# RetNet attention and a multiplicative FFN on one core: attention of the later batches in chunks of 64 positions on array quarters, placed inside the items

## The chip, the core and the metric

The kernel runs on one core of a Trainium2 chip. The metric is the device time of one execution in microseconds. In the text TensorE is PE (PEld: its weight loads), VectorE is DVE, ScalarE is ACT, GpSimd is POOL, and SyncE is SP; PSUM is the accumulator memory, in banks of 2 KB a partition.

## The reference

Everything is float32. Attention has 8 batches, 8 heads, 576 positions and 64 channels a head; the rows of its result go through an FFN with products.

```
scores = q @ k.T / sqrt(64)                     # per batch and head
Dmat   = where(i >= j, gamma[h] ** (i - j), 0)  # decay, gamma[h] = 1 - 2**(-5-h)
x      = ((scores * Dmat) @ v) -> (4608, 512)   # rows: batch, position; columns: head, channel
out    = ((x @ w1) * (x @ w2)) @ w3 @ w_out     # w1, w2: 512x1024; w3: 1024x1024; w_out: 1024x512
```

## The kernel before

**Attention.** Two batches (a pair) go together, and the 576 positions are cut into five chunks: one of 64 and four of 128. A chunk of a pair is a *unit*; there are 20, unit 0 to 4 for the first pair, 5 to 9, 10 to 14 and 15 to 19 for the others. The decay is taken apart: q is multiplied by a power of gamma, v by its inverse (`scale_blocks`, `scale`), so that only a triangular 0/1 mask is left within a chunk, and what earlier chunks give is a running sum over k times v, the *state*. Per unit TensorE has four steps of 16 matmuls each (two batches, eight heads):

- `score` (L233): k times q of the chunk, two heads at once on two halves of the array's rows, into PSUM tiles `sc`; VectorE multiplies them by the mask into `pm` (L236).
- `state` (L255): k times v is added to the PSUM tile `st`, on two halves of the columns; ScalarE copies `st` to SBUF as `sb` (L259), for the next unit. The last chunk of a pair has none.
- `pv_state` (L274): `sb` times q into the PSUM tiles `xps`, on four quarters of the array, 64 by 64 each. The first chunk of a pair has none.
- `pv` (L299): v times `pm` is added to `xps`, on two halves of the columns; ScalarE copies `xps` to the token tile `xT` (L306).

**FFN.** Its products are made by Strassen's scheme. Three kinds of *items* stand in a list `todo`, and `work(n)` issues the next n: `up` (L524, seven products of 8 records of 192 columns; x times w1 and w2 for the first two pairs' tokens), `up2` (L1028, seven of 4 records; two levels of the scheme, for the later pairs, with weight forms that are kept in HBM as `kept` and come back through a ring `ra`), and `down` (L637, seven products of 8 records of 256 columns; the result times w3 times w_out, which was multiplied once before). A matmul in float32 is two records in the trace. GpSimd makes the token forms that `up2` needs (`token_forms`, L948) and some sums (L1033); VectorE adds products up (L1040), multiplies a with b (L1003), and transposes blocks of q and k (L190). `up2` leaves one product outstanding, which `finish` issues inside the next item. An item takes lists of small work with it: `aside` (transposes), `beside` (scaling v on ScalarE), `loads`.

**Order.** The order on every engine is the order of the program; waits come from tiles that are not ready or not free. In the second to fourth pair, some items are issued, then, at the end of a unit, everything of attention at once:

```
pv(g)()                     # pv_state, pv, copies to xT
load(g + 2, "v", ...)       # and k
state(g + 1); score(g + 1)
```

`dealt` says how many items each unit of the third and fourth pair has (3, 4, 4, 3, 3, 7, 7, 3, 7, 7). After units 13, 16 and 19 a group of tokens is complete (`ready`): `finish` and `multiply` close it, and three `down` items of that group follow. PSUM has one bank for `st` and seven for everything else (`acc`), later five and two for `seed`.

Of the kernel before, what the change touches and what calls it, by code (L numbers as in the profile page):

```python
# [19 lines left out]
def kernel(  # L20
# [30 lines left out]
    starts = [0] + [short + c * P for c in range(NC - 1)]  # L51
    G = NB2 * NC
    NB = 3
    TB = S // NB
# [23 lines left out]
    open_attention(att_part)  # L78
    st_ps = ctx.enter_context(tc.tile_pool(name="st_ps", bufs=1, space=PSUM))
    acc_part = ExitStack()  # L80
    acc = acc_part.enter_context(tc.tile_pool(name="acc", bufs=7, space=PSUM))

# [3 lines left out]

    def load(g, names, engine=nc.sync):
        i, c = divmod(g, NC)
        sz = sizes[c]
        src = {"k": k, "q": q, "v": v}  # L90
        for nm in names:
            t = pools["ld"].tile([P, 2 * H, D], F32, tag="ld_" + nm, name="ld_" + nm)
            engine.dma_start(
                t[:sz], src[nm][2 * i:2 * i + 2, :, starts[c]:starts[c] + sz, :].rearrange("b h p d -> p (b h) d"))
            live[nm, g] = t
# [181 lines left out]

    def pv(g):

        if ("xps", g) not in live:  # L280
            pv_state(g)
        i, c = divmod(g, NC)
        sz = sizes[c]
        live["x", g] = True
        vs, pm, banks = live["v", g], live["pm", g], live["xps", g]

        parts = []
        for n in range(NB):
            lo, hi = max(starts[c], n * TB), min(starts[c] + sz, (n + 1) * TB)
            if lo < hi:  # L290
                m = i * NB + n
                if ("xT", m) not in live:
                    live["xT", m] = xps[m % 4 == 3].tile([P, NP, 2, TB], F32, tag="xT", name="xT")
                parts.append((live["xT", m], lo - n * TB, lo - starts[c], hi - lo))
        for m, (b, n) in enumerate(bank_order):
            for r in range(2):
                for half in range(2):
                    p, j = 2 * r + n, half ^ r
                    nc.tensor.matmul(banks[r][heads[half], b, n, :sz], vs[:sz, b * H + 2 * p + j, :],  # L299
                                     pm[:sz, b, j, p, :sz], start=(c == 0 and m == 0), stop=True,  # L300
                                     skip_group_check=True)

        def evict():
            for x, to, fr, n in parts:
                for r in range(2):
                    nc.scalar.copy(  # L306
                        x[:, 2 * r:2 * r + 2, :, to:to + n].rearrange("p n b s -> p b n s"),
                        banks[r][:, :, :, fr:fr + n])

        return evict  # L310

    blocks = [(("A", r, f), None) for f in range(2) for r in range(2)]
# [191 lines left out]
    def up(i, n, fp, conv=0, tail=True, first=False):  # L507
# [20 lines left out]
        def plus(ps, to, sb):  # L528
            nc.vector.tensor_add(c[:, to], ps, c[:, sb])  # L529
            convert(conv.pop(0) if isinstance(conv, list) else conv)  # L530
            for extra in (aside, spread):
                if extra:
                    extra.pop(0)()


        c = ffn.tile([P, 4, 2, TB], F32, tag="c", name="c", bufs=1)
        p1 = product(None, "A11", "B11")
        nc.scalar.copy(c[:, 0], p1)

        convert(owed.pop() if owed else 0)  # L540
# [5 lines left out]
        plus(product(None, "S2", "T2"), 1, 0)  # L546
        plus(p7 if first else product(None, "S3", "T3"), 2, 1)
        p5 = product(None, "S1", "T1")
        plus(p5, 3, 2)
        plus(product(None, "A22", "-T4"), 2, 2)  # L550
        if not first:
            product(p1, "A12", "B21")
        nc.scalar.copy(c[:, 0], p1)
        product(p5, "S4", "B22")
        plus(p5, 1, 1)
# [69 lines left out]
    def down(x, y, then=None, last=False):  # L625
# [34 lines left out]

        C11, C12, C21, C22 = (0, 0), (0, 1), (1, 0), (1, 1)
        product(1, "A11", "B11")
        first = ot[:, 0, 0]
# [4 lines left out]
        if second:  # L668
            store()
            finish()  # L670
        product(7, "S3", "T3")
        if second:
            multiply()
# [7 lines left out]
        nc.vector.tensor_add(ot[:, 0, 1], ps[6], first)  # L681
        nc.scalar.copy(ot[:, 0, 0], ps[2])
        early = second or last or g >= 2 * NC - 1
        if early:
# [8 lines left out]
        if second:  # L693
            store()
        product(3, "S4", "B22", on=5)
        while aside and not early:
# [143 lines left out]
    weights_part.close()  # L840
    open_attention(ctx)
    load(NC, "k")
    load_blocks(NC, "q")
# [77 lines left out]
    def open_second():  # L921
        nonlocal acc
        flush()
        acc_part.close()
        acc = ctx.enter_context(tc.tile_pool(name="acc", bufs=5, space=PSUM, reuse_waits="tile"))
        pools["seed"] = ctx.enter_context(tc.tile_pool(name="seed", bufs=2, space=PSUM, reuse_waits="tile"))
# [81 lines left out]
    def up2(gr, n):  # L1008
# [26 lines left out]
        def plus(ps, j, with_add=None):  # L1035
# [5 lines left out]
            else:  # L1041
                nc.scalar.copy(c[:, j], ps)

        p1 = acc.tile([P, 2, TB], F32, tag="acc", name="up")
        product(p1, "A11", "B11", True)
# [4 lines left out]
        product(p5, "S1", "T1", True)  # L1050
        nc.scalar.copy(c[:, 3], p5)  # L1051
        finish()
        next_forms()
# [10 lines left out]
        product(p1, "A12", "B21")  # L1064
        plus(p1, 0, add)
        product(p5, "S4", "B22")
        if add is not None:
# [11 lines left out]
        if aside:  # L1079
            aside.pop(0)()  # L1080

        def rest():
# [40 lines left out]
    front_blocks(NC, "q")  # L1123
    state(NC)
    score(NC)
    scale_blocks(NC + 1)
    in_blocks = [u >= 2 * NC - 3 for u in range(G)] + [False] * 2
    first_pair = range(NC, 2 * NC - 1)
    for g in first_pair:
        n = (1, 1, 2, 2)[g - NC]  # L1130
        if not in_blocks[g + 2]:
            load(g + 2, "k")
            load_blocks(g + 2, "q")
        scale(g + 1, "v")
        if not in_blocks[g + 1]:
# [14 lines left out]
        work(half)  # L1150
        pv(g)()
        load(g + 2, "v", nc.scalar if in_blocks[g + 2] else nc.sync)
        if in_blocks[g + 2] and (g + 2) % NC != NC - 1:
            load(g + 2, "k")
        state(g + 1)
        score(g + 1)
        if not in_blocks[g + 2]:
# [13 lines left out]
    load_blocks(g + 1, "q")  # L1171
    pv(g)()
    load(g + 2, "v", nc.scalar)
# [17 lines left out]
    load_blocks(g + 1, "q")  # L1191
    state(g)
    score(g)
    add_group(0)
    dealt = [3, 4, 4, 3, 3, 7, 7, 3, 7, 7]
    for g in range(2 * NC, G):
        n = dealt[g - 2 * NC]
        if g + 1 < G:
            beside.extend(lambda j=j: scale(g + 1, "v", range(j, j + H // 2)) for j in (0, H // 2))
            tail = min(n, 4) - 3  # L1200
            work(n - 2 - tail)
            scale_blocks(g + 1)
            if g - 1 in ready:
# [18 lines left out]
        else:  # L1222
            work(n)
        pv(g)()
        if g in ready:
            finish()
            multiply()
        if g + 2 < G:
            load(g + 2, "v", nc.gpsimd)
            if (g + 2) % NC != NC - 1:  # L1230
                loads.append(lambda g=g: load(g + 2, "k", nc.gpsimd))
        if g + 1 < G:
            state(g + 1)
            score(g + 1)
        if g in ready:
            add_group(ready[g])
        if g == G - 1:
            token_forms(ready[g])
    g = G
# [44 lines left out]
```

## Time and profile before

| | |
|---|---|
| time, median of 3 runs | 850.42 us (849.96 to 852.22) |
| time of the profiled execution | 850.68 us |
| its span, first to last instruction | 848.9 us |
| granted TensorE clock, mean | 0.989 |
| busy: PE, DVE, ACT, POOL | 819.3, 541.2, 283.2, 325.6 us |
| second pair's attention (units 5 to 9) | from 234 us on |
| third and fourth pair's attention | from 363 us on |
| last attention step | ends at 705.0 us |

Times in the timeline count from the first instruction. In a row of a group, the array part and the tile that a matmul uses stand before its shape (64\*128: 64 rows, 128 columns of the array); xN is the number of records, then the busy time, the mean length of one in ns, and the idle time of the engine ahead of them, with what ended it.

### The profile page before, as it was taken

To read this page: it belongs to the slowest core of one execution; us is meant where nothing else is said; L and a number is where in the kernel's file an instruction comes from. 1 tells how busy PE (TensorE), PEld (TensorE's weight loads), DVE (VectorE), ACT (ScalarE), POOL (GpSimd) and SP (SyncE) were. 2 spreads that over 40 slices of the span, in tenths; PEclk is the share of its full clock that TensorE was granted. 3 is DMA by queue.
4 is the path that set the end of the run, shared out by engine and by line. 5 is a ranking of instruction groups with operands and counts; after the bars stand their busy time and mean duration, and the time that the engine had idled before them with its cause. 6 is when DMAs were issued, how large, how long until landed. Compare 5 with 4: busy or idle time off the path is not lost.

```text
span 848.9 us, 15774 instructions
## 1 busy us (share of the span) xinstructions
PE 819.3 (97%) x6085; PEld 738.1 (87%) x6085; DVE 541.2 (64%) x887; ACT 283.2 (33%) x581; POOL 325.6 (38%) x330
## 2 busy tenths in 40 slices
PE   7899999999999999979998999999999999999998
PEld 6889999644989998869998889998899998899987
DVE  4899999991644477615657644759735768446653
ACT  4777556670111101033343024342034331033300
POOL 1100010001104181395545935556916468445500
PEclk8999999999999999999999999999999999999999
DMA  9995454436046487979786147787275452245401
GB/s 193 217 224 128 77 150 125 126 98 112 1 98 125 75 220 251 307 209 220 190 229 167 44 93 228 201 238 177 58 156 183 140 208 69 77 148 189 159 25 51
DMA packets 201291, 126.96 MB, mean 150 GB/s; under 512 B 161272, under 2 KB 183032, under 8 KB 201216
## 3 DMA queue, kind: packets, MB, share of 16 engines
q1 hardware_dynamic: 170944, 50.14, 29.1%
q0 software_dynamic: 11776, 63.71, 23.0%
q10 hardware_dynamic: 18496, 12.10, 5.3%
q8 instruction: 48, 0.79, 0.4%
q14 instruction: 27, 0.22, 0.1%
HBM read 103.62 MB, written 22.28 MB: 148 GB/s over the span
## 4 chain that ended last, share of the span: by engine, by line
PE 79%; DMA 7%; DVE 7%; issue 3%; SPq 2%; ACT 1%; POOL 0%; ACTq 0%; DVEq 0%; POOLq 0%
PE po L637 24%; PE up L1028 15%; PE up L524 13%; PE seed L1028 11%; PE ps L477 6%; DMA ld_v<-in_v_dram 3%; PE xps L299 3%; PE sc L233 3%; DMA ra<-kept 2%; PE xps L274 1%; SPq L171 1%; DVE c L529 1%; DVE ab L1003 1%; DMA bl_q<-in_q_dram 1%; PE st L255 1%
## 5 line engine op out<-in xcount | busy, mean ns | idle before, releaser
L637 PE MATMUL po<-w3o,ab 128*128 128x256 f32 x552 | 125.0, 381 | 1.4 <-DVE ot L641 0.5
L637 PEld LDWEIGHTS po<-w3o,ab 128*128 128x128 f32 x552 | 103.9, 190 | 17.4 <-DVE ot L641 1.2
L1033 POOL TENSOR_TENSOR cc<-cc 128x384 f32<-128x384 f32 x112 | 109.3, 1001 | 4.1 <-ACT cc L1051 2.4
L1040 DVE TENSOR_TENSOR cc<-seed,cc 128x384 f32<-128x384 f32 x88 | 48.7, 553 | 72.9 <-PE seed L1028 68.5
L181 POOL TENSOR_TENSOR bl_q<-bl_q,gqs 128x512 f32<-128x512 f32 (+1 forms) x30 | 30.8, 1048 | 127.7 <-DMA bl_q<-in_q_dram 91.8
L939 POOL DMA_DIRECT2D ra<-kept x54 | 30.6, 567 | 124.1 <-PE seed L1028 103.3
L1028 PE MATMUL up<-xT,ra 128*128 128x192 f32 x384 | 74.2, 330 | 0.6 <-DMA ra<-kept 0.6
L1040 DVE TENSOR_TENSOR cc<-up,cc 128x384 f32<-128x384 f32 x88 | 48.4, 550 | 36.8 <-PE up L1028 31.5
L524 PE MATMUL up<-xT,wA 128*128 128x192 f32 x384 | 70.4, 327 | 0.0
L529 DVE TENSOR_TENSOR c<-up,c 128x384 f32<-128x384 f32 x80 | 44.0, 550 | 38.9 <-PE up L524 38.3
L1028 PEld LDWEIGHTS up<-xT,ra 128*128 128x128 f32 x384 | 64.4, 192 | 2.0 <-DMA ra<-kept 0.9
L236 DVE TENSOR_TENSOR pm<-sc,mask 128x512 f32<-128x512 f32 (+1 forms) x80 | 45.4, 626 | 32.1 <-PE sc L233 32.0
L637 PE MATMUL po<-wB,forms 128*128 128x256 f32 x288 | 65.2, 379 | 0.5 <-DVE forms L611 0.5
L524 PEld LDWEIGHTS up<-xT,wA 128*128 128x128 f32 x384 | 63.4, 190 | 1.1 <-issue 0.5
L637 PEld LDWEIGHTS po<-wB,forms 128*128 128x128 f32 x288 | 54.6, 190 | 8.2 <-PE po L637 0.8
L1047 ACT COPY seed<-up 128x384 f32<-128x384 f32 x56 | 25.9, 463 | 100.1 <-PE up L1028 46.6
L1028 PE MATMUL seed<-e,ra 128*128 128x192 f32 x256 | 52.9, 337 | 5.2 <-DVE cc L1040 2.9
L1028 PE MATMUL up<-ra 128*128 128x192 f32 x288 | 55.1, 328 | 1.9 <-DMA ra<-kept 1.9
L477 PE MATMUL ps<-wo,w3T 128*128 128x512 f32 x128 | 55.1, 592 | 0.0
L204 POOL TENSOR_TENSOR ld_v<-ld_v,gk 128x1024 f32<-128x1024 f32 (+1 forms) x9 | 17.1, 1899 | 90.5 <-DMA ld_v<-in_v_dram 90.5
L679 DVE TENSOR_TENSOR ab<-ab,forms 128x512 f32<-128x512 f32 x17 | 17.1, 1008 | 53.3 <-PE po L637 53.3
L1028 PEld LDWEIGHTS seed<-e,ra 128*128 128x128 f32 x256 | 43.7, 194 | 7.8 <-DVE cc L1040 3.6
(127 smaller groups left out, 1597.2 us busy)
## 6 DMA issues: line engine op xcount, KB each, us to landing
ra<-kept POOLq DMA_DIRECT2D x54, 896.0 KB, 5.0
raw<-in_moe_w_dram SPq DMA_DIRECT2D x72, 128.0 KB, 3.0
bl_q<-in_q_dram SPq DMA_DIRECT2D x216, 32.0 KB, 3.2
out_dram<-ot ACTq DMA_DIRECT2D x54, 128.0 KB, 2.3
bl_k<-in_k_dram SPq DMA_DIRECT2D x136, 32.0 KB, 2.4
raw<-in_moe_w_dram SPq DMA_DIRECT2D x16, 256.0 KB, 6.0
ld_k<-in_k_dram SPq DMA_DIRECT2D x8, 512.0 KB, 5.9
raw<-in_moe_w_out_dram SPq DMA_DIRECT2D x32, 128.0 KB, 2.7
```

What stands on the lines that cost most here:

```text
L181: nc.gpsimd.tensor_tensor(out=part, in0=part, in1=gqs[:, :, n0:n0 + n].unsqueeze(3).to_broadcast([P, NP, n, BL]), op=ALU.mult)
L233: nc.tensor.matmul(sc[j][:sz, p, :sz], kT[hs, b, p, :sz], qT[hs, b, p, :sz], start=True, stop=True)
L236: nc.vector.tensor_mul(pm[:sz, b, j, :, :sz], sc[j][:sz, :, :sz], mask[:sz, :sz].unsqueeze(1).to_broadcast([sz, NP, sz]))
L477: nc.tensor.matmul(ps, live["w3T", ft][:, g, :], live["wo"][:, g, :], start=(g == 0), stop=(g == KF - 1))
L524: nc.tensor.matmul(ps[:, w, :], a[:, w, r, :], b[:, r, :], start=(new and w == r == 0), stop=(w == r == 1), skip_group_check=True)
L529: nc.vector.tensor_add(c[:, to], ps, c[:, sb])
L637: nc.tensor.matmul(ps[nm], a[A][:, f, :], live["W"][B][:, f, :], start=(f == 0 and not on), stop=(f == NP - 1), skip_group_check=True)
L939: engine.dma_start(ring[n % 3], kept[n % 14 // 7][nm])
L1028: nc.tensor.matmul(ps[:, w, :], weight_of(slot, a, w), B[b], start=(new and w == 0), stop=True, skip_group_check=True)
L1033: nc.gpsimd.tensor_tensor(out=o, in0=o, in1=i, op=ALU.add)
L1040: nc.vector.tensor_add(c[:, j], ps, with_add[:, j])
L1047: nc.scalar.copy(p6, p1)
```

## The change

From unit 5 on, a unit of 128 positions is treated as two chunks of 64 (`CS`), s = 0 and 1. Every matmul of attention is then 64 rows by 64 columns by 64 positions, and four go to the four quarters of the array. `st` becomes two PSUM banks, one sum for the even chunks and one for the odd ones; what a chunk needs of the state ahead of it is `st[:, 0]`, or that plus a copy `odd` of the odd bank. The last chunk of a pair now has a state step for its first half, and half of its k is loaded for that. For each half of the values, `pv_half`, all sums into one place of PSUM come from the same rows of the array; ScalarE's copy of one column, `hand`, stands between the two halves.

The pieces of a unit no longer stand at the unit's end. `plan` takes them as three: the first half of unit g's values; the second half with the copies and the loads of unit g + 2; the scores and states of unit g + 1. The next item issues them at three places (`begin_item`, `here`). Unit 6 issues its three pieces at once, and unit 9 both halves. `acc` has six banks, later four. v is scaled in quarters instead of halves, at one more place in `up2` and two in `down`. The diff, cut:

```diff
+    st_ps = acc_part.enter_context(tc.tile_pool(name="st_ps", bufs=1, space=PSUM))
...
+    def score2(g):
+        n = (sizes[g % NC] // CS)
+        sc = [acc.tile([P, 2, NP, CS], F32, tag="acc", name="sc") for j in range(2)]
+        for b in range(2):
+            for p in range(NP):
+                for s in range(n):
+                    at_s = slice(s * CS, (s + 1) * CS)
+                    for j, hs in enumerate(heads):
+                        nc.tensor.matmul(sc[j][heads[s], b, p, :], kT[hs, b, p, at_s], qT[hs, b, p, at_s],
+                                         start=True, stop=True)
...
+        for j in range(2):
+            nc.vector.tensor_mul(
+                pm[:sz, j].rearrange("p b m x -> p (b m) x"), sc[j][:sz].rearrange("p b m x -> p (b m) x"),
...
+    def state2(g):
+        n = 1 if c == NC - 1 else (sizes[g % NC] // CS)
+                for s in range(n):
+                    for j, hs in enumerate(heads):
+                        nc.tensor.matmul(st[hs, s, b, p, :], kn[heads[s], h, :], vs[heads[s], h, :],
...
+        def ahead_of(g, s, odd):
+            sb = live["sb", g, s] = pools["fr"].tile([P, 2, NP, D], F32, tag="sb", name="sb")
+            if odd is None:
+                nc.scalar.copy(sb, st[:, 0])
+            else:
+                nc.vector.tensor_add(sb, st[:, 0], odd)
...
+    def state_half(g):
+            for s in range(2):
+                for m, (b, n) in enumerate(bank_order):
+                    for r, j in ((0, 0), (0, 1), (1, 0), (1, 1)):
+                        nc.tensor.matmul(banks[r][heads[j ^ r], b, n, at_s], live["sb", g, s][heads[j], b, p, :],
...
+    def pv_half(g, second):
+        for m, (b, n) in enumerate(bank_order):
+            for r0, s in ((0, 0), (0, 1), (1, 0), (1, 1)):
+                j, r = s ^ second, r0 ^ second
+                    nc.tensor.matmul(
+                        banks[r][heads[half], b, n, s * CS:(s + 1) * CS], vs[heads[s], b * H + 2 * p + j, :],
...
+        if not second:
+            nc.scalar.copy(hand[last[0]], banks[1][last])
...
+    def first_half(g):
+        state_half(g)
+        pv_half(g, False)
+
+    def second_half(g):
+        pv_half(g, True)
+        if ("next", g) in live:
+            live["next", g]()
+        put_x(g)
...
@@ up2
+        begin_item()
         p1 = acc.tile([P, 2, TB], F32, tag="acc", name="up")
         product(p1, "A11", "B11", True)
...
         product(p5, "S1", "T1", True)
         nc.scalar.copy(c[:, 3], p5)
+        here()
         finish()
...
         product(p1, "A12", "B21")
         plus(p1, 0, add)
+        here()
         product(p5, "S4", "B22")
...
         if aside:
             aside.pop(0)()
+        here(8)
+        if beside:
+            beside.pop(0)()
...
@@ down
+        begin_item()
+        here()
         product(1, "A11", "B11")
...
+        here()
         product(7, "S3", "T3")
+        here(8)
...
-        acc = ctx.enter_context(tc.tile_pool(name="acc", bufs=5, space=PSUM, reuse_waits="tile"))
+        acc = ctx.enter_context(tc.tile_pool(name="acc", bufs=4, space=PSUM, reuse_waits="tile"))
...
-        pv(g)()
         if g in ready:
             finish()
             multiply()
-        if g + 2 < G:
-            load(g + 2, "v", nc.gpsimd)
...
+        def rest_and_loads(g=g):
+            second_half(g)
+            if g + 2 < G:
+                load(g + 2, "v", nc.gpsimd)
+                loads.append(lambda: load(g + 2, "k", nc.gpsimd, 1 if (g + 2) % NC == NC - 1 else 2))
+
+        plan.append([lambda g=g: first_half(g), rest_and_loads])
         if g + 1 < G:
-            state(g + 1)
-            score(g + 1)
+            plan[0].append(lambda g=g: scores_and_sums(g + 1))
```

`up` gets the same three places, after its first, third and sixth product.

## The prediction

> **What bounds the kernel now.** I read the page's busy line first, then the chain, then TensorE's groups with shapes apart, and last the timeline around one unit of attention.
>
> ```profile
> PE 819.3 (97%) x6085; PEld 738.1 (87%) x6085; DVE 541.2 (64%) x887; ACT 283.2 (33%) x581; POOL 325.6 (38%) x330
> PE 79%; DMA 7%; DVE 7%; issue 3%; SPq 2%; ACT 1%; POOL 0%; ACTq 0%; DVEq 0%; POOLq 0%
> ```
>
> TensorE is busy 97% and holds 79% of the chain: what counts is TensorE time, and any wait that the change puts before it. The attention rows (x counts records, two to a matmul; the mean is a latency, busy over count is the rate):
>
> ```profile
> L233 PE MATMUL sc<-qT,kT 64*128 64x128 f32 x512 | 35.5, 287 | 4.4 <-ACT qT L221 2.0 <-DVE kT L190 1.7 <-DVE cc L1040 0.7
> L299 PE MATMUL xps<-pm,ld_v 128*64 128x128 f32 x512 | 31.4, 276 | 0.0
> L274 PE MATMUL xps<-qT,sb 64*64 64x128 f32 x512 | 17.7, 275 | 0.0
> L255 PE MATMUL st<-ld_v,ld_k 128*64 128x64 f32 x384 | 13.6, 224 | 0.7 <-POOL ld_v L204 0.7
> ```
>
> L274 already uses four quarters: 35 ns a record against 61 for L299, which uses two halves. One middle unit in the timeline:
>
> ```profile
> 413.94 1.10 PE L274 MATMUL xps<-qT,sb 64*64 64x128 f32 x32
> 414.98 1.97 PE L299 MATMUL xps<-pm,ld_v 128*64 128x128 f32 x32
> 416.77 1.10 PE L255 MATMUL st<-ld_v,ld_k 128*64 128x64 f32 x32
> 417.81 2.06 PE L233 MATMUL sc<-qT,kT 64*128 64x128 f32 x32
> 419.79 0.92 PE L1028 MATMUL up<-xT,ra 128*128 128x192 f32 x4
> ```
>
> From 413.94 to 419.79 the four steps take 1.04, 1.79, 1.04 and 1.98: 5.85 us. VectorE decides a few places. After an item with doubled sums it runs late, here four microseconds behind TensorE, whose item had ended by 542.9:
>
> ```profile
> 540.90 2.73 DVE L1003 TENSOR_TENSOR ab<-cc 128x384 f32<-128x384 f32 x1
> 543.56 1.23 DVE L190 STREAM_TRANSPOSE kT<-bl_k 128x1024 f32<-128x1024 f32 x1
> 546.56 0.53 DVE L1040 TENSOR_TENSOR cc<-up,cc 128x384 f32<-128x384 f32 x1
> ```
>
> **What the Trainium skill says.** "TensorEngine Tiling (Array Packing)", Key Properties: tiles work independently, and a change of tiling mode drains the array. The trace agrees on both: single records of L274 start in fours, 6 to 7 ns apart, every 109 ns, the same 109 in which L299 does two; and a switch costs 0.1 to 0.2 us (below). The same page, Gotcha 1, says that row tiles can't use one PSUM bank at once; L274's four quarters do write two row tiles into each bank, in different halves of the partitions, and lose nothing. "TensorE: Matmul & The Clock Gate", Wait — 56ns, not 53.3ns?, gives a floor of about 25 ns start to start for small matmuls; its Part 3 starts packed tiles about 4 ns apart. The trace has 27 ns a record at most in a long run (L274), set there by N=128, so it doesn't tell which of the two holds for N=64.
>
> **The change part by part.**
>
> *Rates.* Single records: a row of 64 columns comes every 58.3 ns on a tile (L255, two column tiles; L233 at 64x64, two row tiles), 128 columns every 109. Four quarters at N=128 keep the 109 of two, so at N=64 I take 58.3 ns for four records. Each of the four steps (32 matmuls, 64 records) is then 16 x 58.3 = 0.93 us: 3.73 us a unit against 5.85. The bounds of this unknown: 58.3 below (the stream itself), 4 x 25 = 100 above (the skill's floor).
>
> *Switches.* Entering quarters from the FFN costs 0.09 (a record 255 ns after the last instead of 163) and 0.05 on the second group; leaving costs 0.09 and 0.10 (the second FFN record 266 ns later instead of 163). A visit is 0.34. Before: one visit a unit, and three inner switches that stand in the 5.85. After: three visits, 1.02, and inside a visit no change of mode.
>
> *A middle unit* (chunks 1 to 3): 5.85 + 0.2 = 6.05 before, of the visit's cost only what those starts don't hold; 3.73 + 1.02 = 4.75 after: **1.3 us won**. The last chunk gains a state step (64 positions, two tiles, 0.93) and wins 0.4; the short one fills two quarters only, as before.
>
> *Second pair* (units 5 to 9), starts from the timeline. 5 with the scores of 6: 4.4 to 3.8. 6 runs its pieces together, one visit, but the second half waits for ScalarE's one-column `hand` copy (about 0.55, estimated from a small ScalarE copy and two semaphore hops of 0.2): 6.05 to 4.65. 7: 1.3 won. 8: 5.2 to 4.75. Together 3.75. Unit 9 (3.2 to 2.75) and the scores of 10 fall in front of the stretch where TensorE waits 2.25, 1.50 and 1.91 us for GpSimd's token forms and the `ra` loads (gaps at 367.5, 376.2 and 381.3), so they count nothing; those forms hang on SP's `kept` sends from 336.0, which wait for VectorE's L872 inside an earlier item and move with TensorE.
>
> *Third and fourth pair.* Regular places (units 10, 11, 12, 14, 17): 0.4 + 1.3 + 1.3 + 0.4 + 1.3 = 4.7 won. New waits take most of it:
> - `acc` drops from five PSUM banks to four. An up2 item's first half, two products (1.3 us) into the item, needs the bank of the item before, which VectorE frees with its last L1040. Normally that is 1.3 us after the item's end: no wait. Behind units 15 and 18 VectorE is late (546.56 + 0.53 against 544.2 for TensorE; 668.4 against 665.4): 3.0 us each. Queued behind it stand the rest of the item and its scores. Before, those units took 5.5 and 5.7 with the waits of their scores; after 3.0 + 3.8 and 3.1 + 4.75: lost 1.4 and 2.2.
> - At the ends of a group (units 13, 16, 19) the outstanding product needs VectorE; before, values and state ran over that wait (at 585.10 only 0.79 was left), now they stand behind it and TensorE idles to 462.7, 585.0 and 702.8. Followed to the third `down` product (1.73 us each; its operand S2 is VectorE's, behind two pm and one state sum): 474.2 becomes 473.7, 594.9 becomes 596.2, 711.5 becomes 711.2. Won 0.5, lost 1.3, won 0.3.
> Sum: 4.7 - 1.4 - 2.2 + 0.5 - 1.3 + 0.3 = 0.6.
>
> *What lies beside.* VectorE: two pm of 0.63 a unit instead of four, one or two state sums of about 0.65 more: even. ScalarE: the copy of st (0.59) becomes that of its odd bank, `hand` is new, put_x is the same; its 33% hides them, and before the scores 1.3 us (up2) or 1.7 us (down) of products cover put_x's first 0.8. Scaling v in quarters: the same work, two more places. GpSimd: v's load moves from the unit's end behind the second half, past that item's ring load and one sum; it was blocked on TensorE there for 3 us anyway, and from issue to the first scaling stay some 6.7 us (5.8 before: 417.87 to 423.69). The k loads of chunk 9, 14 and 19 (256 KB) are new: one issue on SP, two on GpSimd (1.2 us), in its idle time. Token forms start behind a later put_x by 0 to 5 us; the second and third set ended at 495 and 731 before and were wanted from 510 and 742: covered. The mask copy and the wider st are free.
>
> *Sum:* 3.75 + 0.6 = 4.35 us won. The profiled execution took 850.68 (848.9 span and 1.8 around), 0.26 above the median of 850.42, which I use: **846.0 us**. About 0.3%, 2.6 us, is what can be told from no change.
>
> **The rivals.**
> 1. *Quarters don't keep pace* (slower). The place is every step in quarters: about 720 groups of four records. Each nanosecond over 58.3 costs 0.72 us; from 64.3 ns on the win is gone, from 68 ns the kernel is slower beyond doubt. At the skill's 25 ns a record: 100 ns, +30 us, 876. For it: never more than one PE instruction per 13.7 ns in any run of 64 in this trace, and quarters at N=64 ask for one per 7.3; instruction pages (16 KB, 256 instructions, 0.9 to 1.6 us each on their queue) would last 1.9 us. Against it: bursts of eight in 22 to 28 ns in L274, and 13.7 is where the stream itself binds.
> 2. *New waits eat it*: fewer PSUM banks and the `hand` hop cost some 0.4 us at each of the 28 places that I left free: +11, 857. For it: 3 us at two places already. Against: five of the seven up2 places have VectorE done in time.
> 3. *The second pair's win is absorbed* at 367 to 383, because SP's 22 us of block loads don't move: only 0.6 is left, 850.
> 4. *More is won*: VectorE is less late behind 15 and 18 since pm is halved: 3 to 6 us more, 841.
>
> **How the numbers follow.** My sum 0.42, rival 1 0.22, rival 2 0.16, rival 3 0.12, rival 4 0.08. My sum's own range is 843 to 849, of which a tenth is within 0.3%. Faster: 0.38 + 0.08 = 0.46. Same: 0.04 + rival 3 0.10 + the mild ends of 1 and 2, 0.03 = 0.17. Slower: 0.37. The range 840 to 862 leaves out the upper half of rival 1 and little of 4.
>
> **What would show it.** Right: the four attention lines of pairs two to four at 864, 768, 768 and 864 records, about 1 us of busy time per unit and step, so some 58 us in all where three quarters of all attention rows (113.7 with the 64x64 forms) gave 85; single records every 58 ns in fours; waits of about 3 us for DVE L1040's successor before the first halves of 15 and 18, and idle before the outstanding product at three group ends; no such wait elsewhere. Wrong: a group pitch above 64 ns; waits on ScalarE's `hand` or put_x at many places; gaps at 367 to 383 grown by more than the unit 9 win; a first half that waits for v or k.

## The result and the profile after

The changed kernel takes **895.5 us** (median of 4 runs, 894.6 to 897.4) where the kernel before took 850.2 in the same session: a ratio of 1.053, 95% interval 1.0505 to 1.056. The forecast was 846.0 us with a range up to 862. Its profiled execution spans 892.8 us against 848.9, at a mean TensorE clock of 0.971 instead of 0.989.

The busy line and the chain of the page after:

```profile
PE 819.2 (92%) x7621; PEld 730.9 (82%) x7621; DVE 541.0 (61%) x876; ACT 286.5 (32%) x599; POOL 322.3 (36%) x332
PE 70%; DMA 8%; DVE 8%; issue 6%; SPq 4%; POOL 2%; ACT 1%; ACTq 0%; DVEq 0%; POOLq 0%
```

TensorE's busy time is what it was, though some 27 us of it were meant to go (85 to 58 in the attention rows); its share fell from 97% to 92%. Its share of the chain fell from 79% to 70%, and what it gave up went to `issue`, SP's queue, GpSimd, DMA and VectorE. The four attention rows (shapes apart; records, busy time, mean length, idle time ahead and what ended it):

```profile
L395 PE MATMUL xps<-pm,ld_v 64*64 64x64 f32 x864 | 22.2, 234 | 4.8 <-DVE cc L1173 2.6 <-ACT hand L402 2.2
L350 PE MATMUL st<-ld_v,ld_k 64*64 64x64 f32 x768 | 17.6, 219 | 4.6 <-issue 3.6 <-POOL ld_v L205 1.1
L328 PE MATMUL sc<-qT,kT 64*64 64x64 f32 x864 | 17.3, 221 | 1.6 <-DVE qT L191 1.6
L382 PE MATMUL xps<-qT,sb 64*64 64x64 f32 x768 | 17.1, 246 | 2.6 <-DVE cc L1173 2.6
```

They have the counts that the prediction named, but 74.2 us of busy time in all where it named 58. A busy stretch counts the whole length of its last record, so scores that take 0.98 us from start to start are busy for 1.16; there are more such stretches now, and some records are slow (below). The rows also have waits of their own now. Unit 12, whose three visits lie inside one item, in the timeline (start, us, engine, line, operation):

```profile
441.75 0.66 PE L395 MATMUL xps<-pm,ld_v 64*64 64x64 f32 x30
442.34 1.57 PE L1161 MATMUL seed<-e,ra 128*128 128x192 f32 x8
...
444.49 0.69 PE L395 MATMUL xps<-pm,ld_v 64*64 64x64 f32 x32
445.12 0.92 PE L1161 MATMUL up<-xT,ra 128*128 128x192 f32 x4
...
446.61 1.16 PE L328 MATMUL sc<-qT,kT 64*64 64x64 f32 x64
447.59 1.11 PE L350 MATMUL st<-ld_v,ld_k 64*64 64x64 f32 x64
448.64 0.92 PE L1161 MATMUL up<-xT,ra 128*128 128x192 f32 x4
```

Scores and states take 0.98 and 1.05 us from start to start; with the first visit (440.72 to 442.34) and the second (0.63) the unit's attention is 4.28 us, 4.85 with what the three switches add, against 6.05 before. So the arithmetic of a middle unit is won. TensorE's waits (us in all, times, longest) tell the rest:

```profile
PE up L639 <- DVE c L644: 17.1, 4, 13.8
PE seed L1161 <- DVE cc L1173: 14.0, 5, 3.7
PE po L756 <- DVE forms L730: 4.8, 1, 4.8
PE st L350 <- issue: 3.6, 2, 2.6
PE po L756 <- DVE ot L804: 3.0, 1, 3.0
```

In the kernel before no line of this list is above 3.0 us. To make a balance I summed TensorE's records from 215 us on, each from its start to the next one's, with the time in which no record ran taken out as waits:

| from 215 us on, us | attention | FFN, transposes | waits | sum |
|---|---|---|---|---|
| before | 80.3 | 533.8 | 15.9 | 630.0 |
| after | 65.7 | 545.1 | 63.2 | 674.0 |
| difference | -14.6 | +11.3 | +47.3 | +44.0 |

The distances of single records tell what the +11.3 are, as an estimate: 5.7 lie in the FFN records on either side of a visit to attention, of which there are 42 instead of 19, and 6.7 in FFN records that came slower than usual, most of them at half speed behind a wait; about 1 goes off for records that the trace misses. So of the 14.6 won in attention the switches take 5.7 back.

The waits of after are: 13.8 in one place of the second pair; 10.9 at the three group ends; 10.1 in four places from 370 to 407, where the kernel before has 5.7; 5.3 at units 15 and 18; 5.3 in three stops that the profile calls `issue` (instruction fetch, below); 4.8 behind one sum at unit 14; 2.2 on the `hand` copy; the rest in small ones. The experiments take these in turn. In them the kernel before itself ran between 847 and 863 us, so a run is judged by its ratio to the runs beside it, slow executions left out, and by its trace. The diffs are shown in short.

### The profile page after: what moved, and what is told of

It is laid out like the page before. It is cut to its first block, busy times and chain, and to the rows that moved or that the text cites. A ratio compares the mean times of both kernels' runs of the same rounds, so it can differ in the third digit from the quotient of the medians.

```text
span 892.8 us, 18926 instructions
## 1 busy us (share of the span) xinstructions
PE 819.2 (92%) x7621; PEld 730.9 (82%) x7621; DVE 541.0 (61%) x876; ACT 286.5 (32%) x599; POOL 322.3 (36%) x332
## 4 chain that ended last, share of the span: by engine, by line
PE 70%; DMA 8%; DVE 8%; issue 6%; SPq 4%; POOL 2%; ACT 1%; ACTq 0%; DVEq 0%; POOLq 0%
PE po L756 23%; PE up L1161 13%; PE seed L1161 11%; PE up L639 10%; PE ps L592 6%; SPq L172 3%; DMA bl_k<-in_k_dram 2%; PE xps L395 2%; DMA ld_v<-in_v_dram 1%; DMA out_dram<-ot 1%; PE xps L382 1%; DVE cc L1173 1%; PE sc L328 1%; DVE c L644 1%; PE st L350 1%
## 5 line engine op out<-in xcount | busy, mean ns | idle before, releaser
L756 PE MATMUL po<-w3o,ab 128*128 128x256 f32 x552 | 128.9, 386 | 3.4 <-ACT ot L788 2.6
L1173 DVE TENSOR_TENSOR cc<-seed,cc 128x384 f32<-128x384 f32 x88 | 48.6, 552 | 84.3 <-PE seed L1161 73.7
L182 POOL TENSOR_TENSOR bl_q<-bl_q,gqs 128x512 f32<-128x512 f32 (+1 forms) x30 | 28.6, 976 | 177.8 <-DMA bl_q<-in_q_dram 126.7
L756 PE MATMUL po<-wB,forms 128*128 128x256 f32 x288 | 67.4, 388 | 4.8 <-DVE forms L730 4.8
L802 DVE TENSOR_TENSOR ab<-ab,forms 128x512 f32<-128x512 f32 x17 | 21.0, 1234 | 55.7 <-PE po L756 55.7
L1161 PEld LDWEIGHTS up<-ra 128*128 128x128 f32 x288 | 48.4, 192 | 3.8 <-issue 3.1
L760 DVE TENSOR_TENSOR ot<-po,ot 128x256 f32<-128x256 f32 x72 | 30.3, 421 | 33.4 <-PE po L756 32.6
```

Source lines behind the costliest of these rows:

```text
L182: nc.gpsimd.tensor_tensor(out=part, in0=part, in1=gqs[:, :, n0:n0 + n].unsqueeze(3).to_broadcast([P, NP, n, BL]), op=ALU.mult)
L756: nc.tensor.matmul(ps[nm], a[A][:, f, :], live["W"][B][:, f, :], start=(f == 0 and not on), stop=(f == NP - 1), skip_group_check=True)
L760: nc.vector.tensor_add(ot[:, to[0], to[1]], ps[nm], ot[:, sb[0], sb[1]])
L1161: nc.tensor.matmul(ps[:, w, :], weight_of(slot, a, w), B[b], start=(new and w == 0), stop=True, skip_group_check=True)
L1173: nc.vector.tensor_add(c[:, j], ps, with_add[:, j])
```

## The experiments

### The 13.8 us of the second pair

The changed kernel, on VectorE and TensorE, and GpSimd's queue ahead of it:

```profile
299.21 2.29 POOL L182 TENSOR_TENSOR bl_q<-bl_q,gqs 128x512 f32<-128x512 f32 x2 [16.25 <-DMA bl_k<-in_k_dram]
301.44 3.21 POOL L1015 DMA_DIRECT2D kept<-wA  x4
296.75 14.95 SPq L172 DMA_DIRECT2D bl_k<-in_k_dram  x16
324.73 1.25 DVE L191 STREAM_TRANSPOSE kT<-bl_k 128x1024 f32<-128x1024 f32 x1 [15.00 <-DMA bl_k<-in_k_dram]
328.06 2.93 PE L639 MATMUL up<-xT,wS 128*128 128x192 f32 x8 [13.79 <-DVE c L644]
```

SP fetches unit 9's k in 16 pieces from 296.75; GpSimd's sends of kept weights, 256 and 768 KB each, start 4.7 us later and share the DMA engines. The transpose waits 15 us for k, the sum `c` stands behind it on VectorE, TensorE behind the sum. In the kernel before:

```profile
300.63 1.90 POOL L204 TENSOR_TENSOR ld_v<-ld_v,gk 128x1024 f32<-128x1024 f32 x1 [19.44 <-DMA ld_v<-in_v_dram]
302.50 3.76 POOL L181 TENSOR_TENSOR bl_q<-bl_q,gqs 128x512 f32<-128x512 f32 x2
306.21 0.96 POOL L882 DMA_DIRECT2D kept<-wA  x1
```

There v's scaling, which waits for its load, stands ahead of the sends on GpSimd's queue; they start 8.4 us behind the first piece of k (SP, 297.79). The change puts that scaling behind the items. First this alone, in the kernel before:

```diff
-        scale(g + 1, "v")          # ahead of the items
         work(half)
+        scale(g + 1, "v")
         pv(g)()
```

> The kernel before, with one line moved as the change moves it: in the second pair v of the next unit is scaled on GpSimd behind the unit's items instead of ahead of them. Everything else, the halves of the array and the end of the unit included, stays. Theory A (GpSimd's scaling held back the sends of the kept weights until SP's blocks of k for unit 9 were in; without it both share the DMA engines and the blocks come late): a TensorE wait of over 8 us near 310 that ends on VectorE behind the transpose kT<-bl_k, and 858 to 866 us. Rival B (the 14 us wait comes from the pieces in the items or from the loads of v and k that they issue): no such wait, within 1.5 us of 850. Rival C (the whole loss lies in the quarters): the same, 850.

Measured: 0.997 of before (0.994 to 1.000), no wait above 0.4 us near 312. Theory A as I had put it fell. The sends still started 7.2 us behind the first piece (306.00 and 298.83): GpSimd scales unit 9's blocks of q next, and those landed late, beside v's load of 512 KB (296.96). Next the other side, the changed kernel with later sends:

```diff
-            todo.extend([*ups[:2], forms[0], *ups[2:], forms[2], (flush,), forms[1], ...
+            todo.extend([*ups[:3], forms[0], *ups[3:], forms[2], (flush,), forms[1], ...
```

> The changed kernel, with the first sends of kept weights one up item later in the list (behind the third up item of the second pair instead of the second). Theory A: SP's blocks of k have the DMA engines to themselves, the transpose kT<-bl_k ends some 13 us earlier, TensorE's wait of 13.8 us goes and with it the half clock behind it: 895.5 less 13.8 to 16, so 879.5 to 882; a part may be lost again where the kept weights are wanted (near 399). Rival B (the wait comes from the pieces or their loads): the wait stays, 894 to 897.

Measured: 1.038 (1.031 to 1.044). The wait fell from 13.8 to 3.8 us. So the sends were what k met. How many there are counts, and not only when they start: here too the first went out 3.8 us behind the first piece of k (305.95 and 302.11), but only five before 319.32, where the changed kernel sends 15 by 313.25. What let so many go early was still to be shown. The change also issues v's load later, in the second place of an item, so blocks of q land sooner. Both moves together, in the kernel before:

```diff
         work(half)
+        scale(g + 1, "v")          # and not ahead of the items
         pv(g)()
-        load(g + 2, "v", ...)
+        # for unit 9: issued in the next up item, behind its third product
```

> The kernel before with two lines moved as the change moves them: v of the next unit is scaled behind the unit's items (as in the first run), and the load of unit 9's v (512 KB) is issued in the next item, behind its third product, instead of at the end of unit 7. The halves of the array and all else stay. Theory A, mended (two things held GpSimd's first sends of kept weights back: the scaling, and the v load that shared the DMA engines with the blocks of q which GpSimd scales next; with both gone the sends start some 5 us behind the first block of k instead of 7 to 8): the sends start before 303, the transpose kT<-bl_k is late and TensorE waits 4 to 14 us near 312, 1.005 to 1.016 of before. Rival B (the places of the pieces themselves make the wait): none above 2 us there, within 0.3% of before.

Measured: **1.0134** (1.0101 to 1.0166), with the old attention and its old places. The two lines that matter:

```profile
300.30 1.72 POOL L886 DMA_DIRECT2D kept<-wA  x2
323.67 2.61 PE L526 MATMUL up<-xT,wS 128*128 128x192 f32 x7 [9.29 <-DVE c L531]
```

The sends start 3.7 us behind the first piece (296.63), TensorE waits 9.3 us. Two moves, one harmless by itself, make the wait without a single quarter; the load's move alone wasn't run. And the changed kernel with its second pair at the unit's end again:

```diff
+        scale(g + 1, "v")          # ahead of the items, as before
-        plan.append(turn)
+        for piece in turn:
+            piece()
```

> The changed kernel with its second pair as in the quarters at the unit's end (scaling ahead of the items, pieces and loads at the end of units 5 to 8); the third and fourth pair stay as changed. Theory A (the second pair's loss is the meeting of the sends with the blocks of k, which the moved scaling and the moved load of v bring about): no wait near 314, the second pair within 3 us of the kernel before's, what is left, 20 to 27 us over before, is the third and fourth pair's: 1.023 to 1.032 of before. Rival B (the quarters make the wait in whatever place): 1.045 to 1.055.

Measured: 1.036 (1.030 to 1.042), no such wait. The second pair's order is thus worth about 0.017 of 1.053, some 15 us (9 to 20 by the two intervals); what stays is more than I expected by 0.004.

### Group ends, and the clock behind a wait

At units 13, 16 and 19 TensorE waits 3.7, 3.7 and 3.5 us for the outstanding product. The first test puts the values back ahead of it:

```diff
+        if g in ready:             # and the later sends of above
+            first_half(g); second_half(g)
         if g in ready:
             finish()
             multiply()
```

> As the run with later sends, and besides, for units 13, 16 and 19, both halves of the values at the unit's end, ahead of the outstanding product, and the last token forms straight behind them, as in the kernel before. Theory A2 (at the three group ends TensorE stands 3.5 to 3.7 us for VectorE because nothing covers the outstanding product; then it runs at half clock): three waits of 3.6 shrink below 1 and some 0.5 us of slow records each go: 10 to 13 us under the run with later sends. Rival E (the halves only move; what the products wait for is VectorE's queue, which ends at the same time): the waits turn up behind the outstanding product, within 4 us of the run with later sends.

Measured: 1.032 (1.025 to 1.039); the interval overlaps that of the run with later sends. In the traces the three waits fell to 1.2, 1.2 and 1.0 us and one of 4.9 at unit 14 (below) was gone, but from the same point of unit 12 to the end it is only 2.3 us shorter: 10 us of waits on VectorE's and ScalarE's work are new, for the scores' `kT` (1.7) and within the `down` items (`ab` 1.8, `ra` 1.6, `ot` 3.4, `forms` 1.5). By the trace rival E was right: most of a group end is VectorE's queue, and moving TensorE's work ahead of it only shifts where TensorE meets it. The second test fills the wait with work that does nothing:

```diff
         if g in ready:
+            keep_busy(15)          # 30 records of 128 columns
             finish()
```

> The changed kernel with 15 idle matmuls of 128 by 128 (30 records, about 3.3 us) ahead of the outstanding product at the three group ends, where TensorE waits 3.5 to 3.7 us for VectorE. They fill the wait and do no useful work. Theory K (half of what a wait of this length costs comes behind it: records at half speed): the wait shrinks to under 0.5 us, and behind it the 64 records of a state step take 0.95 us instead of 1.4 to 1.76, the 32 of the first values 0.42 instead of 0.77; 0.9 to 1.3 us won at each of the three, about 3 us, 1.047 to 1.052 of before. Rival L (the slow records come from the switch into quarters or from late operands): the records behind are as slow as they were, no gain or some loss.

The same stretch behind the first group end, in the changed kernel and then with the fill:

```profile
489.03 0.92 PE L1161 MATMUL seed<-e,ra 128*128 128x192 f32 x4 [3.71 <-DVE cc L1173]
489.88 1.74 PE L382 MATMUL xps<-qT,sb 64*64 64x64 f32 x64
491.37 1.10 PE L395 MATMUL xps<-pm,ld_v 64*64 64x64 f32 x32
492.40 2.59 PE L756 MATMUL po<-w3o,ab 128*128 128x256 f32 x8
```

```profile
488.28 0.92 PE L1161 MATMUL seed<-e,ra 128*128 128x192 f32 x4 [0.37 <-DVE cc L1173]
489.13 1.16 PE L382 MATMUL xps<-qT,sb 64*64 64x64 f32 x64
490.11 0.65 PE L395 MATMUL xps<-pm,ld_v 64*64 64x64 f32 x32
490.69 1.99 PE L756 MATMUL po<-w3o,ab 128*128 128x256 f32 x8
```

The wait ends at the same moment, but behind it the state step takes 0.98 instead of 1.49 us, the first values 0.58 instead of 1.03. From the state step to the second `down` product's end it is 6.03 against 7.59 us; 1.57 and 1.40 are won at the other two ends, 4.5 in all, somewhat more than theory K expected. The ratio, 1.044 (1.037 to 1.052), doesn't resolve that by itself. "TensorE: Matmul & The Clock Gate", Part 1, says that an idle window of about 3.4 us halves TensorE's clock; these waits of 3.5 to 3.7 us, and this cure, agree. Shorter waits did it here too (last section).

### The 4.8 us at unit 14

VectorE's sum for the first `down` item, and what GpSimd did beside it:

```profile
500.49 5.69 DVE L730 TENSOR_TENSOR forms<-ab 128x512 f32<-128x512 f32 x1
499.89 1.95 POOL L1081 TENSOR_TENSOR ra<-xT 128x384 f32<-128x384 f32 x2
501.80 3.83 POOL L1081 TENSOR_TENSOR ra<-xT,ra 128x384 f32<-128x384 f32 x4
506.33 1.19 PE L756 MATMUL po<-wB,forms 128*128 128x256 f32 x2 [4.84 <-DVE forms L730]
```

The token forms ran on at 0.96 to 0.98 us each; the sum took 5.69 us, and TensorE's next ten records came every 427 ns instead of 216. "SBUF — State Buffer", SBUF: two separate sides, says that VectorE with two SBUF operands and a GpSimd operation that reads SBUF exclude each other for a whole instruction. To see whether that is the cause, GpSimd was made to wait for VectorE's sums:

```diff
         if g - 1 in ready:
+            nc.gpsimd.tensor_copy(out=seen, in_=<S1 of the first down item>[:, 0, :2])
             token_forms(ready[g - 1])
```

> The changed kernel with one small GpSimd copy of two columns of VectorE's last sum (S1) ahead of the token forms at units 14 and 17, so that the forms start behind the sums that the first down item wants. Theory M (at unit 14 VectorE's sum L730, of two SBUF operands, stood 5.69 us because GpSimd's token forms, which read SBUF too, went on back to back; TensorE waited 4.84 us for it and then ran ten records at half clock): the sum takes 0.7 to 1 us, the wait near 501 falls below 1.5 us, the ten records take 216 ns instead of 427, 5 to 6.5 us won, 1.044 to 1.048 of before; the forms end 2 to 3 us later, still ahead of the up2 items. Rival N (the sum is long for another reason, such as its own operands): the sum stays above 4 us and the wait with it, 1.05 to 1.055.

```profile
503.29 0.68 DVE L731 TENSOR_TENSOR forms<-ab 128x512 f32<-128x512 f32 x1
504.13 3.04 PE L757 MATMUL po<-wB,forms 128*128 128x256 f32 x13
```

The sum took 0.68 us, the wait was gone, and from the `up2` items of unit 12 to those behind the group's `down` items the kernel was 7.2 us shorter. Theory M holds. The total, 1.048 (1.044 to 1.052), is at the edge of what theory M put, and its interval overlaps that of the changed kernel (1.0505 to 1.056): 4 us were given back in the next `up2` items, where a fetch wait of 2.91 us (2.63 in the changed kernel, which kept its clock) was followed by some six microseconds of records at 320 ns instead of 162.

The same meeting stands behind a wait further up. At 374.67 VectorE's sum L802 took 6.05 us beside GpSimd's forms, and TensorE waited 3.03 us for what follows it (381.12). In the trace of the kernel before this sum (L679, 355.81) took 1.62 us. But where only v's scaling was moved, without a quarter, it took 5.97 us (359.35), so it takes no quarters for this to happen.

### The quarters alone, and instruction fetch

The quarters with everything at the unit's end, as in the kernel before:

```diff
-        plan.append([lambda g=g: first_half(g), rest_and_loads])
-            plan[0].append(lambda g=g: scores_and_sums(g + 1))
+        first_half(g)
+        second_half(g)
         ...                        # finish, multiply, loads where they were
+        scores_and_sums(g + 1)
```

> The quarters alone: chunks of 64 on four quarters, two banks of st, acc of 6 and then 4 banks as in the change, but all pieces at the unit's end and all scaling and loading of v where the kernel before has them. Theory (the arithmetic in quarters is worth what the prediction said, and the loss is one of order): a middle unit takes 3.7 us for its four steps and 0.3 to 0.6 for the hand copy, against 5.85; about 1.5 us won at 11 units, 0.4 at the others: 836 to 842 us. Rival D (256 instructions in 3.7 us are more than the instruction fetch brings, 16 KB a page): each of those units waits 1 to 2.6 us, 845 to 865. Rival C (the quarters themselves lose the time): above 870.

Measured: 1.023 (1.014 to 1.031); the trace gives 65.5 for attention, 535.5 for the rest, 45.4 of waits. Neither my 836 to 842 nor rival C; rival D comes nearest, though its 865 is passed, and fetch is only a part: 7.9 us of the waits are `hand` copies, 6.7 us are `issue`, and all but one of these stops end 2.3 to 2.6 us after the queue of instructions started a page of 16 KB (at 423.48 in the case below, whose stop ends at 426.11). Half a page more of instructions, early in the kernel:

```diff
     def keep_busy(n):
+        # at its first call only: 32 matmuls of 4 columns, 128 instructions
```

> The quarters at the unit's end, with 32 small matmuls more (128 instructions of TensorE, half a page of 16 KB) near 10 us, long before any of the places in question. Theory F (TensorE's waits on nothing that the profile shows, 6.7 us of issue in six places from 271 on, are its instruction fetch: pages run out in the densest bursts): the places at which they fall move by half a page, so most of the six bursts that waited (units 6, 7, 11, 12, 17) don't and others do; the sum stays between 3 and 10 us and the time within 4 us but for the 2 us added. Rival G (those waits belong to the steps: a switch, a semaphore that the trace misses): the same six places wait for the same time.

Measured: 1.033 (1.023 to 1.044). Unit 11 without and with the shift:

```profile
423.27 0.76 PE L328 MATMUL sc<-qT,kT 64*64 64x64 f32 x36
426.11 0.62 PE L328 MATMUL sc<-qT,kT 64*64 64x64 f32 x27 [2.08 <-issue]
```

```profile
443.31 1.11 PE L332 MATMUL sc<-qT,kT 64*64 64x64 f32 x64
444.25 0.74 PE L354 MATMUL st<-ld_v,ld_k 64*64 64x64 f32 x35
446.86 0.69 PE L354 MATMUL st<-ld_v,ld_k 64*64 64x64 f32 x29 [1.87 <-issue]
```

The stop moved from behind record 36 of the scores to behind record 35 of the states: 63 records, 126 instructions, the half page to within a record. Unit 12's went from scores to states likewise (1.17 and 1.96 us), units 7 and 8 from states to scores. Theory F holds for these; the two stops of 0.7 us behind unit 18 stayed, and the trace puts them on VectorE. The shift cost far more than 2 us: some 10 were lost ahead of the region looked at, and a stop of 4.2 us came up at unit 8. How long a stop lasts differs from run to run.

### Can the quarters win with another order?

Four orders were tried. Two take the quarters at the unit's end and let the scores go into the next item:

```diff
         first_half(g)
+        state2(g + 1)              # v_between; in v_spread it goes into the next item
         second_half(g)
+        plan.append([..., lambda g=g: score2(g + 1)])
```

> The quarters at the unit's end, rearranged: the state step of the next unit stands between the two halves of the values, where TensorE waited 7.9 us in all for the hand copy; the scores of the next unit stand in the next item, behind its first product in the second pair and its fifth in the later ones; sb has three buffers, so that the sum ahead of the next unit is made at once. Theory H (hand copies and scores behind late VectorE sums and transposes cost 14 us of the quarters at the unit's end; the fetch 6.7): 10 to 14 us under those, 0.995 to 1.010 of before. Rival F (the fetch is what limits: four steps in a row, 384 instructions in 2.9 us, now wait longer for it): issue waits grow above 12 us, within 4 us of the quarters at the unit's end.

> As the run with the state step between the halves, but that step goes into the next item too, ahead of the scores: bursts of 256, 128 and 128 instructions instead of 384 and 128. Rival F: issue waits fall below 3 us, and it is the faster of the two although the hand copy is uncovered again (0.4 us a unit, some 7 in all). Theory H: the issue waits were small, and it is 3 to 7 us slower than the other.

1.010 (1.002 to 1.019) and 1.014 (1.007 to 1.021). From 215 to 760 us the state step between the halves cut `hand` from 7.9 to 2.2 us and raised `issue` from 6.7 to 9.2; spread out, `issue` was 1.6 and `hand` 7.9 again. Each did what its theory said, and the two cancel: neither F nor H decides.

> A try at a faster kernel. The second pair in quarters at the unit's end; in the third and fourth pair the first half of the values stands at the unit's end, the second half with the next unit's states behind the second product of the next item (two products cover the hand copy), the scores behind its fifth; at the three group ends both halves stand ahead of the outstanding product. sb has three buffers. Theory I (attention itself gives back 14.6 us; what eats it is 7.9 us of hand copies, 7 to 9 us of instruction fetch in bursts of 384 to 512 instructions, and the first halves' wait for banks behind units 15 and 18, all of which this order avoids in the later pairs): 3 to 8 us under before, 0.990 to 0.997. Rival J (each place that is emptied finds the next wait on VectorE or ScalarE right behind it, since TensorE waits little in the kernel before because everything ends just in time): no faster than the run with the state step between the halves, 1.005 to 1.015.

```diff
         first_half(g)              # third and fourth pair
+        plan.append([lambda: (second_half_and_loads(), state2(g + 1)), lambda: score2(g + 1)])
```

1.013 (1.008 to 1.018). Units 12 and 13 came out ahead: from the last `up2` item ahead of unit 12's end to the last `down` products of the first group it took 66.3 us, 69.2 in the kernel before. From unit 10's values to unit 12's it was even (48.7 and 48.6). Behind the first group it lost: 2.6 and 1.7 us for banks behind units 15 and 18, 2.7 and 1.6 where the ring comes late.

> A second try at a faster kernel, from the first one's waits: in the second pair the state step stands between the two halves and the scores go into the next item (as in the earlier run); for units 15 and 18, behind which VectorE is late, all but the scores stands at the unit's end, 2.9 us of cover for the next item's banks; the load of the next ring slot is issued ahead of v's load on GpSimd. Theory I: of the first try's waits those on VectorE at units 15 and 18 (4.3 us), on the ring (5.7) and half of those on the hand copy (2.3) go: 8 to 11 us under it, 0.990 to 1.002 of before. Rival J (the next wait stands right behind): within 4 us of the first try, 1.008 to 1.015.

```diff
+        if g in (15, 18):          # all but the scores at the unit's end
+            state2(g + 1); second half and loads
-        here(); finish(); next_forms()
+        finish(); next_forms(); here()
```

**1.0089** (1.0064 to 1.0114), the best of the quarters and still slower than before. Its attention is 61.8 us, 18.5 less than before's, its waits 34.3 and its other records 544.7: the waits on banks and ring fell from 10.0 to 4.2 us, those on VectorE at the outstanding products (5.6 to 7.1), on `ab` and on `forms` grew. Rival J holds as far as these orders go. No order of the quarters was found that beats the kernel before.

## Why the prediction was wrong

The time lost against the kernel before, in us, between equal points of TensorE's FFN work (named by their times in the kernel before; one profiled execution each):

| | 238 to 350, second pair | 350 to 427 | 427 to 478, first group end | 478 to 598, second | 598 to 715, third |
|---|---|---|---|---|---|
| changed kernel | 16.1 | 10.8 | 7.5 | 5.3 | 4.3 |
| its second pair at the unit's end | 2.9 | 9.3 | 8.9 | 8.9 | 4.3 |
| all quarters at the unit's end | 1.3 | 6.4 | 1.7 | 5.4 | 1.3 |
| no quarters, scaling and load moved | 10.4 | 8.5 | -1.6 | 0.3 | 0.0 |

- **Rates** were right: 64 records in 0.91 to 0.98 us where 0.93 was predicted, and no fall of the pace in bursts but for the stops. Rival 1 in its own form (a pitch above 64 ns) is out.
- **Switches and a middle unit** were right: 4.85 us for unit 12 where 4.75 was predicted, 1.2 won for 1.3. Attention won 14.6 us from 215 us on.
- **Second pair**: 3.75 us predicted as won. This failed, and the step is "What lies beside". There the scaling of v was called the same work at more places, and v's load was followed in the later pairs alone. In the second pair both stand ahead of, or beside, what releases GpSimd's sends; I cost their move at nothing without naming what queued behind them. In place of the win it lost 16.1 us; the order is worth some 15 (0.017), of which 13.8 are one wait. I had named SP's later sends (from 336.0), as a thing that moves with TensorE, but not GpSimd's, which moved against SP's loads. Nor did the quarters win there when kept at the unit's end (1.3 lost).
- **Group ends**: the idle time was foreseen as a place, but the sum (+0.5, -1.3, +0.3) failed. It followed TensorE to the third `down` product with every record at full speed and VectorE's sums and products at their usual length. At that product the change had lost 5.8, 2.7 and 4.1 us since the last equal point ahead of the group end. The missing terms are the half clock at all three (1.4 to 1.6 us each, shown by the fill), and at the first S2, the third product's operand, beside the token forms (4.8 us, and the ten slow records behind it; shown by forms first). At the third, VectorE's product L1136 took 3.67 us beside GpSimd's sums (739.94) where it took 0.55 in the kernel before (L1003, 699.98), and TensorE's idle time lasted 2.8 us longer than I had put it; no run tests that cause.
- **Units 15 and 18**: 3.0 us of waiting each predicted, 2.65 measured (1.95 + 0.70 and 1.96 + 0.69), on the named line of VectorE. Right.
- **`hand`**: predicted 0.55 at unit 6, measured 0.47; at unit 9 it was 1.70.
- **The unit 9 win absorbed at 367 to 383**: it went further; the waits there grew from 5.7 to 10.1 us. Runs without quarters and with another second pair showed waits of like size in that stretch, and the run without quarters lost 8.5 of the 10.8 us there, so how much of that is the change's stays open.
- **Rival 1's half sentence on instruction pages** was the right thing in the wrong form: the mean rate suffices, and single bursts of some 250 instructions and more still stop, 5.3 us in the changed kernel, up to 9.2 in the orders tried.
- **Rival 2** had the direction (new waits eat the win), but 0.4 us at 28 places isn't what happened: five causes, each at one to four places.

## What to carry to other kernels

When a step is moved, list what stood behind it on its queue: a scaling that waits for a load can be what keeps a large transfer off someone else's loads, and its price is that transfer's. Where an engine is 97% busy and everything arrives just in time, a win of 18 us in one part of its arithmetic can be lost to the next wait of each other engine; look first at whether those have slack. A wait of 3.5 to 3.7 us on TensorE cost 1.4 to 1.6 us more behind it.

## What the runs showed of the hardware

- Four quarters with 64 columns keep 64 records in 0.91 to 0.98 us, 14 to 15 ns a record, for as long as instructions are there.
- Dense bursts outrun the instruction fetch. 64 records with their weight loads are 128 instructions in about a microsecond. The changed kernel has 3,072 matmul and weight-load instructions more than the kernel before and fetches 12 pages of 16 KB more (60 for 48), so a page is 256 instructions; its packets take 0.9 to 1.7 us. The changed kernel's four stops (0.4 to 2.6 us) each end 2.5 to 3.0 us after such a page is started.
- The length of a wait alone doesn't decide on the clock. In the changed kernel 1.71 us without a record, up to 421.81, were followed by 3.41 us at a granted clock of 0.5; 2.63 us, up to 589.86, were followed by the full clock, and 2.91 us at the same place in another run by the half. The stretches at 0.5 last 3.41 us or a multiple, and in the changed kernel all begin on one grid of that step (381.01, 401.49, 421.97, 490.24 and so on). It may be that the place of a wait on this grid decides as well; that fits these cases, but no run tests it.
- VectorE's sum stood through some six GpSimd operations in a row (5.69 us for 0.68), not one; at unit 17 the same pair of engines took turns (0.85 us). The page cited tells of the exclusion for a whole instruction, not that a row of them can hold the other engine off.
